# One kernel for a linear-attention recurrence, top-1 experts and a SwiGLU: first units and tail rearranged, the old state added by TensorE

## The chip, the core and the metric

The kernel runs on one core of one Trainium2 chip. What counts is the time of one execution on the device in microseconds (us). Five engines work side by side, each through its own instructions in program order: TensorE (PE in the profile, its weight loads PEld), VectorE (DVE), ScalarE (ACT), GpSimd (POOL) and SyncE (SP), whose queue issues most transfers. An instruction waits on semaphores for what it reads, and for the buffer that it writes.

## What is computed

Three layers in a row, for 2 batches of 768 tokens, in float32:

```
for t in range(S):                                   # attention, per batch and head (8 heads of 48)
    cur = einsum('bhd,bhe->bhde', u * k[t], v[t])
    y[t] = einsum('bhd,bhde->bhe', r[t], state + cur)
    state = w[t][..., None] * state + einsum('bhd,bhe->bhde', k[t], v[t])
x = y as 1536 rows of 384
expert = argmax(x @ w_gate)                          # top-1 of 8 experts, with a capacity, in token order
x = gate * (relu(x[expert] @ w1) @ w2)               # each expert 384 -> 1024 -> 384
out = (silu(x @ w_gate2) * (x @ w_val)) @ w_out      # 384 -> 1536 -> 384
```

## The kernel before

The recurrence is done in 12 units of 128 tokens, six to a batch (`UPB`). In a unit the products of the decays take two directions from the middle: `X` are running products and `R` running sums that stand for inverse products, started anew at every eighth token from `anch`, reciprocals of X. For unit u:

- `prep0` (ScalarE): copies of the decay `wm`, one place shifted, from the unit's load `dm`.
- `prep1` (VectorE): two scans X (L363), then two reciprocals `anch` (L368).
- `prep2` (VectorE): two scans R (L406), the products `M` of k and r with X and with R (L412, L415), and in `prep3` the product `rk` of r and k (L425).
- `scores`: eight matmuls `psA` of M with M (L460), two copies to `A` on ScalarE (L462), two masks on GpSimd (L463).
- `kgtok`: k of M transposed into `psT`, copied to `kgt` (L471, L473).
- `values`: y = A times v, plus M times the state `Sb` (L485, L490).
- `state`: eight matmuls P = kgt times v (L502); d, the decay of the whole unit (L505); `Sa` = P + old state (L510), except in a batch's first unit; `Sc` = Sa times d (L513). `expand` copies Sc into `Sb` on ScalarE (L521).
- `own` (GpSimd): `aV` = v times the diagonal term of the unit (L440). The diagonal comes from `rk` and u by matmuls in `gate_t`, a copy on ScalarE and `columns` (L570, L572).
- `xrow` (VectorE): x = y + aV (L527). `gate_t` transposes x for the gate.

The order is written out by hand (`manual_schedule`), one unit after the other. The loop's round u works on several units at once: `xrow(u - 1)`, `state(u)`, `scores(u + 1)`, `prep1(u + 2)`, `prep2(u + 2)`, `values(u)`, `own(u + 1)`. The input `dm` has three buffers, so `load_dm(u + 4)` in round u waits on SyncE's queue for rk of unit u + 1. `tick` puts one pending small step of the expert choice behind a VectorE instruction, and `flush` all of them. `warm(n)` is n bf16 matmuls whose result nobody reads.

The tail handles units 10 and 11 and the last groups of the choice: `four` (units 4 to 7), `two` (8, 9) and `last` (10, 11). For a group: logits, `choose` (largest, one-hot, exponentials and their sum), `count` (places within an expert by matmuls), `place`, then the rows weighted (`xg`) and scattered to the experts' places in HBM (`scatter`, GpSimd, L735). The first expert's rows of the last units don't take that way: `onehot` and `x0_add` (L810) sum them into PSUM by matmuls with a one-hot, where `x0_load` has brought what earlier units scattered. Of units 8 and 9 the weighted rows go in as float32, of 10 and 11 as two float32r halves (`x0_high` on ScalarE, `x0_low` on VectorE). `fill(us)` puts as many pieces of the weights' conversion into halves as `us` allows (ScalarE L207, VectorE L212). `early.close()` ends the buffers of the recurrence, behind which `load_raws` may load three more weight pieces.

## Time and profile before

| | us |
|---|---|
| median of 3 runs | 473.61 (472.63 to 474.22) |
| profiled execution | 477.16 |
| its span | 475.4 |
| PE busy | 454.4 (96%) |
| DVE busy | 335.0 (70%) |
| ACT busy | 239.8 (50%) |
| POOL busy | 72.6 (15%) |

The span runs from the first to the last instruction of the profiled execution. Busy shares are averages over stages that differ: the recurrence and the choice come first, then the experts (from 108.9 us), then the SwiGLU. In the chain of work that ended last, PE has 79% of the span and DVE 10%. PEclk is the granted clock of TensorE as a share of its upper level; "idle before" in brackets is how long the engine stood before an instruction, with what ended it.

### The profile page before, as it was taken

What the parts mean: (1) busy time and instruction counts of PE and PEld (TensorE: products, weight loads), DVE (VectorE), ACT (ScalarE), POOL (GpSimd) and SP (SyncE); (2) the same over time, 40 slices, a digit from 0 to 9 for tenths busy, and PEclk for the clock granted to TensorE, in tenths of its full rate; (3) what the DMA queues carried; (4) which work ended last, traced back from release to release, by engine and by line L of the source; (5) the groups of instructions that cost most, each with busy time, mean ns of one, the idle gap of its engine ahead of it and who ended that gap; (6) DMA issues with size and microseconds to landing.
All of it is one profiled execution on the core that took longest, in us unless ns stands there. A gap on an engine that the chain in (4) does not pass through costs nothing.

```text
span 475.4 us, 9312 instructions
## 1 busy us (share of the span) xinstructions
PE 454.4 (96%) x3572; PEld 401.8 (85%) x3572; DVE 335.0 (70%) x723; ACT 239.8 (50%) x560; POOL 72.6 (15%) x87
## 2 busy tenths in 40 slices
PE   7899889888999999999999999999999999999994
PEld 3587668678999999999988888888888888888884
DVE  8889999677798658559779966575868576434241
ACT  4466676636788677665455465353625333221220
POOL 3334445621000000000000370000000000003033
PEclk9899998959999999999999999999999999999999
DMA  7877996564989965027323425042200000001011
GB/s 241 234 236 205 361 270 186 184 215 135 293 272 345 305 239 175 24 67 219 115 77 123 71 64 122 11 123 77 66 2 1 1 0 0 1 0 68 0 68 66
DMA packets 33649, 62.57 MB, mean 132 GB/s; under 512 B 5216, under 2 KB 16992, under 8 KB 33600
## 3 DMA queue, kind: packets, MB, share of 16 engines
q1 hardware_dynamic: 31680, 57.20, 39.2%
q0 software_dynamic: 1920, 4.73, 2.7%
q8 instruction: 29, 0.48, 0.4%
q14 instruction: 20, 0.16, 0.1%
HBM read 52.48 MB, written 9.44 MB: 130 GB/s over the span
## 4 chain that ended last, share of the span: by engine, by line
PE 79%; DVE 10%; issue 4%; ACT 2%; DMA 2%; POOL 1%; another core or an unknown queue 0%; POOLq 0%; SPq 0%; DVEq 0%; ACTq 0%
PE psg L1381 31%; PE psu L1404 14%; PE psh L1270 14%; PE pso L1288 14%; DVE R L406 2%; DVE X L363 1%; PE psA L460 1%; DMA scr<-zrow 1%; POOL out L1416 1%; DVE M L415 1%; DVE M L412 1%; PE psx L1255 1%; PE y L490 1%; PE psW L449 1%; DVE rk L425 1%
## 5 line engine op out<-in xcount | busy, mean ns | idle before, releaser
L1381 PE MATMUL psg<-yb,wu 128*128 128x512 f32 x648 | 156.3, 395 | 0.0
L1381 PEld LDWEIGHTS psg<-yb,wu 128*128 128x128 f32 x648 | 121.5, 188 | 26.0
L1404 PE MATMUL psu<-wu,a 128*128 128x384 f32 x432 | 80.8, 336 | 0.0
L1404 PEld LDWEIGHTS psu<-wu,a 128*128 128x128 f32 x432 | 76.4, 188 | 2.9
L1270 PE MATMUL psh<-xe,wu 128*128 128x240 f32 x576 | 69.1, 277 | 1.4 <-DVE xe L816 1.4
L1270 PEld LDWEIGHTS psh<-xe,wu 128*128 128x128 f32 x576 | 66.2, 190 | 1.7 <-issue 1.6
L1288 PE MATMUL pso<-h,wu 128*128 128x240 f32 x576 | 66.4, 275 | 0.0
L1288 PEld LDWEIGHTS pso<-h,wu 128*128 128x128 f32 x576 | 65.3, 190 | 0.0
L1388 DVE TENSOR_TENSOR t<-t,psg 128x512 f32<-128x512 f32 x36 | 24.7, 686 | 52.6 <-PE psg L1381 35.6
L212 DVE TENSOR_TENSOR wu<-raw,wu 128x512 fp32r<-128x512 f32 x96 | 61.7, 683 | 0.0
L207 ACT CAST wu<-raw 128x512 fp32r<-128x512 f32 x96 | 55.0, 620 | 3.1 <-PE pso L1288 1.4
L1393 ACT CAST a<-t 128x512 fp32r<-128x512 f32 x36 | 22.3, 618 | 58.2 <-DVE t L1388 55.9
L1277 DVE SCALAR_TENSOR_TENSOR h<-psh,h 128x240 fp32r<-128x240 f32 x64 | 25.0, 403 | 24.1 <-ACT h L1276 23.8
L1303 POOL DMA_INDIRECT idl<-ids,dests x12 | 13.5, 1122 | 163.6 <-DVE bits L187 160.3
L1416 POOL DMA_INDIRECT out<-acc,idc x12 | 11.7, 973 | 174.1 <-DVE acc L1414 172.3
L207 ACT CAST wu<-bits 128x384 fp32r<-128x384 f32 x36 | 18.0, 514 | 40.0 <-DVE bits L200 39.2
L1387 ACT ACTIVATE t<-psg 128x512 f32<-128x512 f32 x36 | 21.4, 596 | 27.5 <-PE psg L1381 27.5
L1394 DVE TENSOR_TENSOR a<-t,a 128x512 fp32r<-128x512 f32 x36 | 24.8, 689 | 11.7 <-ACT a L1393 11.0
L1276 ACT ACTIVATE h<-psh 128x240 fp32r<-128x240 f32 x64 | 23.2, 372 | 11.0 <-PE psh L1270 10.2
L1414 DVE TENSOR_TENSOR acc<-psu,acc 128x384 f32<-128x384 f32 x24 | 12.9, 558 | 20.8 <-PE psu L1404 20.8
L462 ACT COPY A<-psA 128x512 f32<-128x512 f32 x24 | 12.9, 588 | 25.3 <-PE psA L460 23.0
L463 POOL TENSOR_SCALAR_AFFINE_SELECT A<-A 128x512 f32<-128x512 f32 x24 | 19.5, 834 | 27.5 <-ACT A L462 27.5
(153 smaller groups left out, 566.9 us busy)
## 6 DMA issues: line engine op xcount, KB each, us to landing
raw<-in_moe_w SPq DMA_DIRECT2D x32, 768.0 KB, 9.0
dm<-in_dm SPq DMA_DIRECT2D x18, 291.0 KB, 6.1
scr<-zrow SPq DMA_DIRECT2D x12, 384.0 KB, 5.4
raw<-in_moe_w_gate SPq DMA_DIRECT2D x6, 768.0 KB, 5.9
raw<-in_moe_w_val SPq DMA_DIRECT2D x6, 768.0 KB, 4.3
raw<-in_moe_w_out SPq DMA_DIRECT2D x6, 768.0 KB, 4.3
v<-in_tk SPq DMA_DIRECT2D x12, 192.0 KB, 6.7
dm<-in_dm SPq DMA_DIRECT2D x3, 512.0 KB, 5.7
```

Of the source, the lines that this page charges most:

```text
L207: nc.scalar.copy(out=slot_t[u % NSLOT][:, 0, c:c + n], in_=bits[i])
L212: nc.vector.tensor_tensor(out=w[:, 1, c:c + n], in0=bits.pop(i), in1=R(w[:, 0, c:c + n]), op=ALU.subtract)
L1270: nc.tensor.matmul(ps, w[:, a, k, c0:c0 + 128], xet[e][:, b, k, :], start=n == 0, stop=n == 8)
L1276: nc.scalar.activation(out=h[:, 0, :], in_=ps, func=AF.Relu)
L1277: nc.vector.scalar_tensor_tensor(out=h[:, 1, :], in0=ps, scalar=0.0, in1=R(h[:, 0, :]), op0=ALU.max, op1=ALU.subtract)
L1288: nc.tensor.matmul(ypt[e, d], w[:, a, f % 4, 128 * d:128 * d + 128], h[:, b, :], start=f == 0 and n == 0, stop=f == 7 and n == 2)
L1381: nc.tensor.matmul(gps[i][g], w[:, a, g, k, c0:c0 + 128], yb[t, k][:, c], start=a_ == k == 0, stop=a_ == k == 2)
L1387: nc.scalar.activation(out=t, in_=pg[0], func=AF.Silu)
L1388: nc.vector.tensor_tensor(out=t, in0=t, in1=pg[1], op=ALU.mult)
L1393: nc.scalar.copy(out=a[:, 0], in_=t)
L1394: nc.vector.tensor_tensor(out=a[:, 1], in0=t, in1=R(a[:, 0]), op=ALU.subtract)
L1404: nc.tensor.matmul(out_ps[t, j], att[i][:, c, 128 * j:128 * j + 128], w[:, a, f % 4, :], start=f % FP == 0 and n == 0, stop=f % FP == FP - ...
```

## The change

- `state`: the old state is added in PSUM by a matmul with the identity as the first into P; `Sa` is gone, and Sc reads P.
- `prep1` ends with X; the reciprocals are one instruction over both halves, in a function of its own, `anchored`.
- In a round, `prep0(u + 2)` and `prep1(u + 2)` come first, then `xrow(u - 1)`, `state(u)`, `anchored(u + 2)`.
- `own(u)` stands behind `scores(u + 1)`, in place of `own(u + 1)` at the round's end; `expand(u)` behind `gate_t`.
- Round 0: `values(0)` in one piece, then the diagonal of units 0 and 1 by two matmuls of 8 columns and one copy.
- Tail: `own(10)` on GpSimd behind the masks of unit 11; the first `fill` ahead of `own(11)`; `early.close()` and the loads behind it after `x0_load`; units 8 and 9 as float32r halves; the weighted rows, places and scatters of `two` later; the second `fill` behind `offsets`; two warming matmuls.

```
@@ prep1
-        A = halved(anch[u % 2], HC)
-        for h in range(2):
-            nc.vector.reciprocal(out=anchors(A, h, G - 1), in_=anchors(X, h, G + 1))
-            tick()
+    def anchored(u):
+
+        if u >= NU:
+            return
+        nc.vector.reciprocal(out=each8(anch[u % 2], HC), in_=each8(Xf[u], XW))
+        tick()
@@ state
+        if u % UPB:
+            nc.tensor.matmul(P, ident, Sc[u], start=True, stop=False, skip_group_check=True)
         for p in range(NP):
             for g in range(2):
                 c0 = D * (2 * p + g)
                 nc.tensor.matmul(P[64 * g:64 * g + 64, p, :], k[:, p, 64 * g:64 * g + 64], vts[u][:, c0:c0 + D],
-                                 start=True, stop=True, skip_group_check=True)
+                                 start=not u % UPB, stop=True, skip_group_check=True)
...
-        src = P
-        if u % UPB:
-            src = ap2.tile([128, NP, D], F32, tag="Sa", name="Sa")
-            nc.vector.tensor_tensor(out=src, in0=P, in1=Sc[u], op=ALU.add)
-            tick()
         s = Sc[u + 1] = ap2.tile([128, NP, D], F32, tag="Sc", name="Sc")
-        nc.vector.tensor_tensor(out=s, in0=src, in1=d.unsqueeze(2).to_broadcast([128, NP, D]), op=ALU.mult)
+        nc.vector.tensor_tensor(out=s, in0=P, in1=d.unsqueeze(2).to_broadcast([128, NP, D]), op=ALU.mult)
@@ the loop
         chosen, counted = ended.get(u - 2), ended.get(u - 3)
+        if u:
+            prep0(u + 2)
+            prep1(u + 2)
         xrow(u - 1)
         state(u)
-        if u:
-            prep0(u + 2)
+        anchored(u + 2)
         warm((7, 4)[u] if u < 2 else 3, ps1, "xT")
         scores(u + 1)
-        expand(u)
+        if u:
+            own(u)
         kgtok(u + 1)
-        if u:
-            prep1(u + 2)
...
+        expand(u)
         load_dm(u + 4)
...
             values(u)
             columns(u - 1, max(u - 2, 0), u + 1)
-            own(u + 1)
         else:
-            values(u, [0, 1])
+            values(u)
             for q in range(2):
-                columns(q, q, q)
-                own(q)
-            values(u, [2, 3])
+                to = logits_to(q)
+                nc.tensor.matmul(to[:, 0:E], gss.pop(q), fold[:, E:2 * E], start=True, stop=True)
+            a8 = gp.tile([128, 2, H], F32, tag="a82", name="a82")
+            nc.scalar.copy(out=a8, in_=lgt[group[0]][:, 0:2, 0:E])
+            for q in range(2):
+                a8s[q] = a8[:, q, :]
+            own(0)
@@ the tail
     scores(u + 1)
+    own(u)
...
-    early.close()
-    more_raws(RAWS[2])
-    load_raws(len(raws_))
     values(u, [2])
...
     xrow(u)
+    fill(1.2, 3.0)
     rows4[2]()
     own(u + 1, nc.vector)
...
     x0_load()
+    early.close()
+    more_raws(RAWS[2])
+    load_raws(len(raws_))
...
-    fill(1.2, 3.0)
     values(u + 1, [3])
-    for f in rows2:
-        f()
+    for i, q in enumerate(two):
+        x0_high(q, sm2[:, i, :])
     xrow(u + 1)
     logits(u)
+    warm(2)
...
-    x0_add(xgs[two[0]], R(hot[0][:, 0, :]), 0, first=True, ks=[0])
+    x0_add(xhl[two[0]][0], hot[0][:, 0, :], 0, first=True)
+    for i, q in enumerate(two):
+        x0_low(q, sm2[:, i, :])
+    for f in rows2:
+        f()
     judge()
...
     logits(u + 1)
-    for f in later:
-        f()
-    for q in two:
-        scatter(q)
-    flush()
-    fill(0.6, 3.0)
-    x0_add(xgs[two[0]], R(hot[0][:, 0, :]), 0, first=True, ks=[1, 2])
+    x0_add(xhl[two[1]][0], hot[0][:, 1, :], 0)
+    for i, q in enumerate(two):
+        x0_add(xhl[q][1], hot[0][:, i, :], 0)
...
     for f in (*bases, *sums):
         f()
+    flush()
+    for f in later:
+        f()
+    for q in two:
+        scatter(q)
...
-    x0_add(xgs[two[1]], R(hot[0][:, 1, :]), 0)
...
     offsets(one8)
+    fill(0.6, 3.0)
```

What that makes of the instructions' order. VectorE, from the cast of tri in round 0 to the R scans of unit 3 (the number behind wm and anch is the buffer's), before:

```order
L898 CAST tri<-before 128x128
L527 TENSOR_TENSOR x<-y,aV 128x384
L505 TENSOR_TENSOR d<-X 128x4
L510 TENSOR_TENSOR Sa<-psP,Sc 128x192
L513 TENSOR_TENSOR Sc<-Sa,d 128x192
L363 SCALAR_TENSOR_TENSOR X<-dm_110,xinit 128x264 x2
L368 RECIPROCAL anch_114<-X 128x32 x2
L406 SCALAR_TENSOR_TENSOR R<-wm_116,anch_114 128x256 x2
```

and with the change:

```order
L902 CAST tri<-before 128x128
L363 SCALAR_TENSOR_TENSOR X<-dm_110,xinit 128x264 x2
L527 TENSOR_TENSOR x<-y,aV 128x384
L510 TENSOR_TENSOR d<-X 128x4
L513 TENSOR_TENSOR Sc<-psP,d 128x192
L371 RECIPROCAL anch_114<-X 128x2x32
L409 SCALAR_TENSOR_TENSOR R<-wm_116,anch_114 128x256 x2
```

The two X scans moved ahead of x and the state, Sa is gone, and the reciprocal is one. The later units stand in the same order.

GpSimd, from the masks of unit 1 to those of unit 3 (A are the masked scores; the number behind a is the buffer of the diagonal), before:

```order
L463 AFFINE_SELECT A<-A 128x512 x2
L440 TENSOR_TENSOR aV<-v,a_355 128x384
L440 TENSOR_TENSOR aV<-v,a_360 128x384
L463 AFFINE_SELECT A<-A 128x512 x2
L440 TENSOR_TENSOR aV<-v,a_479 128x384
L463 AFFINE_SELECT A<-A 128x512 x2
```

and with the change:

```order
L466 AFFINE_SELECT A<-A 128x512 x2
L443 TENSOR_TENSOR aV<-v,a_361 128x384
L466 AFFINE_SELECT A<-A 128x512 x2
L443 TENSOR_TENSOR aV<-v,a_361 128x384
L466 AFFINE_SELECT A<-A 128x512 x2
L443 TENSOR_TENSOR aV<-v,a_472 128x384
```

The product aV is now that of the unit of the running round, one unit later than before, and is issued straight behind the masks of the next unit.

## Rows read from the trace of the kernel before

**Rows 1.** Busy us by engine (instructions), granted clock, DMA share, GB/s, in three stretches

```profile
50.00:60.00 10.00, 9.18 (x167) 7.10 (x165) 10.00 (x29) 7.58 (x21) 4.03 (x5) 1.00 1.03 355
60.00:70.00 10.00, 8.72 (x145) 6.38 (x141) 9.97 (x23) 7.76 (x25) 3.93 (x5) 1.00 1.07 273
96.00:104.00 8.00, 6.85 (x35) 5.68 (x36) 6.41 (x31) 3.32 (x9) 0.97 (x1) 0.50 0.63 216
```

**Rows 2.** VectorE's timeline, one unit: start us, us, engine, line, operation, tiles, shapes

```profile
36.29 0.55 DVE L527 TENSOR_TENSOR x<-y,aV 128x384 f32<-128x384 f32 x1
...
37.00 0.34 DVE L510 TENSOR_TENSOR Sa<-psP,Sc 128x192 f32<-128x192 f32 x1
37.38 0.36 DVE L513 TENSOR_TENSOR Sc<-Sa,d 128x192 f32<-128x192 f32 x1
37.66 1.30 DVE L363 TENSOR_TENSOR_SCAN X<-dm,xinit 128x264 f32<-128x264 f32 x2
38.87 0.54 DVE L368 RECIPROCAL anch<-X 128x32 f32<-128x32 f32 x2
39.33 1.70 DVE L406 TENSOR_TENSOR_SCAN R<-wm,anch 128x256 f32<-128x256 f32 x2
...
42.14 0.68 DVE L425 TENSOR_TENSOR rk<-dm 128x512 f32<-128x512 f32 x1
```

**Rows 3.** TensorE's timeline, the same unit

```profile
35.62 0.67 PE L502 MATMUL psP<-v,kgt 128*64 128x48 f32 x16
...
39.22 0.55 PE L541 MATMUL psx<-ident,x 128*128 128x128 f32 x3
...
41.75 0.67 PE L502 MATMUL psP<-v,kgt 128*64 128x48 f32 x16
```

**Rows 4.** Timeline of the first units, TensorE and VectorE; idle time before in brackets

```profile
18.35 0.40 PE L570 MATMUL lg<-fold,gs 128*128 128x16 f32 x2 [1.24 <-ACT gs L886]
...
21.49 0.56 DVE L527 TENSOR_TENSOR x<-y,aV 128x384 f32<-128x384 f32 x1 [1.72 <-POOL aV L440]
...
24.61 1.25 DVE L406 TENSOR_TENSOR_SCAN R<-wm,anch 128x256 f32<-128x256 f32 x2
...
29.35 0.56 DVE L527 TENSOR_TENSOR x<-y,aV 128x384 f32<-128x384 f32 x1 [1.27 <-PE y L490]
...
30.21 0.36 DVE L510 TENSOR_TENSOR Sa<-psP,Sc 128x192 f32<-128x192 f32 x1 [0.23 <-PE psP L502]
```

**Rows 5.** Timeline of GpSimd and VectorE, three places

```profile
47.71 0.98 POOL L440 TENSOR_TENSOR aV<-v,a 128x384 f32<-128x384 f32 x1 [0.83 <-ACT a L572]
...
47.92 1.31 DVE L415 TENSOR_TENSOR M<-dm,R 128x512 f32<-128x512 f32 x1
...
73.21 1.22 POOL L463 TENSOR_SCALAR_AFFINE_SELECT A<-A 128x512 f32<-128x512 f32 x2 [1.15 <-ACT A L462]
```

**Rows 6.** Timeline of the tail, TensorE, VectorE and ScalarE

```profile
89.18 0.84 PE L565 MATMUL lg<-wgs,xT 128*128 128x8 f32 x6
...
90.54 0.56 DVE L440 TENSOR_TENSOR aV<-v,a 128x384 f32<-128x384 f32 x1 [1.01 <-ACT a L572]
...
92.13 1.12 ACT L207 CAST wu<-raw 128x512 fp32r<-128x512 f32 x2
...
95.04 0.17 DVE L695 TENSOR_TENSOR t<-lg,ohs 128x16 f32<-128x16 f32 x1 [2.28 <-remote]
95.34 1.28 DVE L212 TENSOR_TENSOR wu<-raw,wu 128x512 fp32r<-128x512 f32 x2
...
97.15 0.90 PE L541 MATMUL psx<-ident,x 128*128 128x128 f32 x3 [3.50 <-DVE x L527]
...
97.63 0.17 DVE L680 COPY pcs<-lg 128x16 f32<-128x16 f32 x1
...
98.67 1.45 PE L565 MATMUL lg<-wgs,xT 128*128 128x8 f32 x6
...
108.89 1.27 PE L1270 MATMUL psh<-xe,wu 128*128 128x240 f32 x9 [1.40 <-DVE xe L816]
```

More of the change, by code (lines that the diff above doesn't have):

```diff
@@ L845, in build @@
     prep1(0)
+    anchored(0)
     make_identity(nc, ident)
@@ L859, in build @@
     prep1(1)
+    anchored(1)
     prep2(1)
@@ L967, in build @@
     values(u + 1, [1, 2])
-    c2, sums2, rows2, _ = chosen_of(two)
+    c2, sums2, rows2, sm2 = chosen_of(two)
     for f in c2:
```

## Prediction

> **What bounds the kernel now.** I read the engines' busy time by stretch first. While the recurrence runs over its twelve units, VectorE has no idle time left: 10.00 of 10 us from 50 to 60 and 9.97 from 60 to 70, while TensorE has 9.18 and 8.72 [rows 1]. The experts and the SwiGLU begin at 108.89 [rows 6] and are left alone by the diff. So what can move is the first 109 us: the units, and the tail from the last state to the first expert matmul.
>
> Next the order of time on VectorE in one unit [rows 2]: x of the unit before at 36.29, the state's three steps (d, Sa, Sc), the two X scans, two reciprocals (anch), two R scans, two products M, and rk at 42.14, behind which the next x comes at 42.8. That is 6.5 us with no gap. TensorE in the same unit goes from its state product at 35.62 to the next at 41.75: 6.13 us, also without a gap [rows 3]. The two are 0.4 us apart. A VectorE saving is worth what it takes only as long as TensorE, the masks on GpSimd and the loads don't come due first.
>
> Then the first units, which do wait [rows 4]: x of unit 0 waited 1.72 us for GpSimd's v*diagonal, because TensorE stood 1.24 us for ScalarE's copy of the diagonal rows (and then for the copied diagonal); x of unit 1 waited 1.27 us for y, and the sum behind it 0.23.
>
> **The change, part by part.**
>
> *First units.* Unit 0's values are now issued in one piece ahead of the diagonal, the diagonal of units 0 and 1 takes one copy, and VectorE runs X of unit 3 before it asks for x of unit 0. Where it stood from 19.77 to 21.49 VectorE would go on with X (37.66 to 38.87 in the later unit, 1.21), x 0.47, d about 0.15, Sc 0.36, anch 0.46 and reach R of unit 3 at 19.77 + 2.65 = 22.4, against 24.61 now [rows 2, 4]. If the load of that unit is not there yet the gain shrinks to nothing at the worst; I take 2.0. The wait of 1.27 + 0.23 in the next unit goes too, since TensorE, no longer held by the diagonal, is earlier there by more than that: 1.5. Together **3.5 us**.
>
> *The old state on TensorE.* Sa took VectorE 0.38 us from its start to that of Sc (37.00 to 37.38, [rows 2]). It goes from eight units; one lies inside the 2.0 above, so 7 x 0.38 = 2.7. Sc now reads the sum in PSUM itself; in unit 0 it already does and takes 0.36, as with Sa, so nothing is added. TensorE gets one more f32 matmul of 192 columns per unit. The trace has none; three of 128 columns against the same identity take 0.55, which makes 0.28 for 192, and the whole state product of eight takes 0.67 [rows 3]. Between these I take 0.3, near the lower end, the row with the same operand. TensorE's unit becomes 6.13 + 0.3 = 6.4 us. Four of the nine units are shorter for it (no state or no transposes at the batch's border), and without its own early waits [rows 4] it starts the run of units further ahead of VectorE than now, so I cost the 0.3 at nothing while VectorE is late; without that cover it would cost up to 7 x 0.3 = 2.1.
>
> *One reciprocal for two.* Two of 32 columns take 0.46 from the first's start to R's [rows 2]. One of 64 has the same elements and one start-up less. Between 0 and 0.23 per unit; I take 0.06, since the time seems to go with elements: 8 x 0.06 = **0.5**.
>
> *X ahead of row add and state.* It removes no work. What it buys is cover: 1.2 us of VectorE work stand between rk and the first thing that needs TensorE. In the steady units there is no wait to cover, so I count it at nothing there. Queued behind a late X are now x, the state and, on ScalarE, the masks' copies, since the copies of the decay for that unit are moved up with it.
>
> *v*diagonal behind the masks.* On GpSimd the product now follows the two masks directly instead of coming some 3 us after them. Nobody waits for it sooner: x of that unit is asked for a unit later. But it is where I expect to lose something. VectorE's M at 47.92 took 1.31 us, where rk, a product of the same size, takes 0.68 at 42.14, and it did so while v*diagonal ran on GpSimd (47.71 to 48.69) [rows 2, 5]: the 0.54 from GpSimd's end to M's end is about one product. M seems to have stood until GpSimd was done. The R pair at 39.33 lost 0.45 the same way to the masks (1.70 against 1.25 at 24.61, [rows 2, 4]). About 0.6 us per unit is lost so now. Put behind the masks, the product falls beside R and M, where it used to fall partly beside x and the state, which lost little. I take 0.3 more per unit, between 0 and the 0.98 of a whole product: 8 x 0.3 = **2.4 us lost**.
>
> [...]
>
> Units in all: 3.5 + 2.7 + 0.5 - 2.4 = **4.3 us** earlier at the last state.
>
> *Tail.* (a) Two weight halves of 1.28 us leave the path in front of x of unit 11 and move to the 1.01 us in which VectorE waits for the last diagonal [rows 6]: -1.2, and +0.2 where they don't fit. Their next two casts on ScalarE (1.12 us) then stand ahead of the exponentials of the same group, whose sum VectorE asks for next: +0.6. Net -0.4. [...] If it now keeps the clock (two warming matmuls are put there), -1.0. (c) The one-hot sums of units 8 and 9 become single-pass products that are done before the last group's one-hot exists, so the last ones start with it: -0.7, and the count is not behind them: -0.3. (d) Six small VectorE steps such as the copy of pcs (0.17, the next begun 0.1 behind it, [rows 6]) now stand between the last exponentials and the last places: +0.6 less the 0.2 that VectorE waited there. Sum between -0.2 (if the clock was never low in a run without the profiler) and -2.0; I take **-1.2**. The weight loads that were freed at 87 now queue on SyncE behind the read-back of the first expert's rows. The experts convert those loads some 20 us after they begin, so I cost this at nothing; if that cover went, they would be waited for.
>
> **What the sum is made against.** The profiled execution took 477.16 us, 475.4 of it the span, 3.55 above the median of 473.61. It holds a wait of 2.28 us at 95.04 for which the trace names no instruction [rows 6], and half clock behind it. I don't count on that wait in the median, nor on its going. So 4.3 + 1.2 = 5.5 is taken from the median: **468.1 us**.
>
> **Rivals.**
> 1. *No added collision, and the tail gives all.* 3.5 + 2.7 + 0.5 + 2.0 = 8.7: 464.9. For it: half of the collisions are a matter of phase, and the phase shifts anyway.
> 2. *The loads come due.* From 50 to 70 the DMA engines are at a share of 1.03 and 1.07, full [rows 1]; a unit's inputs are asked for when the unit three before is done with the buffer. If the transfers from 50 us on can only come 2 us earlier, X of unit 11 waits and with it ScalarE and the masks: units give 2.0, tail 1.2: 470.4. The 0.3 on TensorE coming due (2.1) gives 470.2, the same.
> 3. [...] With three GpSimd instructions in a row, each can stop VectorE for its whole length: two masks 1.22 (73.21) and a product 0.98 [rows 5] are 2.2 per unit against the 0.6 lost now, +1.6 x 9 = 14.4. Less 6.7 + 1.2 saved: 480.1. It decides from +0.9 per unit on. [...]
> 4. *No change.* The units end earlier and the tail gives it back, at the read-back and the row scatters in front of the experts: 473.6.
>
> **Chances.** Forecast 0.48, rival 1 0.20, rival 2 0.18, rival 3 0.08, rival 4 0.06. The range leaves out rival 3 and the far ends: 463.8 to 472.5. A difference under about 0.3% (1.4 us) can't be told from none here. Faster by more: 0.86 (forecast, rivals 1 and 2); within: 0.06; slower: 0.08.
>
> **What would show it.** In the trace of the changed kernel: R of unit 3 at about 22.5, no wait of x in units 0 and 1; Sc of the last state some 4.3 us earlier than now; x to x in a unit about 6.3; v*diagonal beside R or M with these at 1.3 rather than 0.7. A wait of X for its load would show rival 2, TensorE without a gap while VectorE waits for the state product its second half. The first expert matmul should stand near 103, or near 101 if the nameless wait is gone. [...]

## The result and the profile after

| us | before | changed |
|---|---|---|
| median | 473.75 (472.63 to 474.22) | 477.35 (477.04 to 477.99) |
| profiled execution, its span | 477.16, 475.4 | 477.18, 475.5 |
| last M of unit 11 begins | 83.13 | 78.49 |
| x of unit 11 | 96.54 | 88.74 |
| first expert matmul | 108.89 | 100.61 |
| first h of the experts | 110.25 | 108.42 |
| first expert matmul to the end of the span | 366.5 | 374.9 |

The changed kernel is **slower: ratio 1.0081, interval 1.0060 to 1.0102**. Forecast was 468.1. The two profiled spans are equal although the medians are not: the profiled execution of before took 3.4 us more than its median, and it holds the nameless wait of 2.28 us [rows 6] with a granted clock of 0.50 behind it [rows 1]. A trace of the old loop and tail without that wait (the run before_late, below, which defers the loads too) has the last M at 81.63, x of unit 11 at 92.86 and the first expert matmul at 105.06. Against it the changed kernel is 3.1, 4.1 and 4.45 us ahead. So in this pair of traces the part that the change works on became 4.45 us shorter, of 5.5 that were forecast, and **8.4 us were lost behind it**, in a stage that the prediction left alone.

That stage at its start. TensorE's timeline (start, us, tiles, count; in brackets the idle time ahead and what ended it):

```profile
100.61 4.30 PE L1284 MATMUL psh<-xe,wu 128*128 128x240 f32 x36 [1.15 <-ACTq L1223]
109.28 1.21 PE L1284 MATMUL psh<-xe,wu 128*128 128x240 f32 x4 [4.37 <-DVE h L1291]
```

The first four groups of nine matmuls run, fill the four buffers of `psh`, and TensorE stands, because nobody takes the results away. ScalarE's row, and the waits of 100 to 112 us (engine, line, what it waited for: total, times, longest):

```profile
108.42 0.37 ACT L1290 ACTIVATE h<-psh 128x240 fp32r<-128x240 f32 x1 [8.56 <-SPq L1223]
```

```profile
ACT h L1290 <- SPq L1223: 8.6, 1, 8.6
DVE h L1291 <- ACT h L1290: 8.5, 1, 8.5
```

The releaser is neither a matmul nor a load but SyncE's queue at L1223, the conditional block of the rare path that is not taken. What SyncE had in flight there, from its own timeline:

```profile
92.81 2.12 SPq L169 DMA_DIRECT2D raw<-in_moe_w  x4
108.73 0.82 SPq L1259 DMA_DIRECT2D xr<-scr  x2
```

What SyncE did at L1223 (duration in ns, smallest, median and largest; first and last start in us), and what it waited there in total, times, longest:

```profile
L1223 SPq EVENT_SEMAPHORE  x9: 17/17/17, 97.8 to 108.3; - x9
L1223 SPq COMPARE_BRANCH  x1: 70/70/70, 97.3 to 97.3; - x1
```

```profile
SPq L1223 <- SPq L1223: 10.6, 5, 3.0
```

The compare-and-branch itself took 0.07 us at 97.3. What held SyncE are the nine semaphore instructions that the program has behind it on the same line: they start between 97.8 and 108.3, and their waits end as the four deferred weight loads land, at 100.0, 103.0, 105.8 and 108.2 (the third by SyncE's semaphore, for its landing is not in the trace). SyncE issues its next transfer at 108.73. In the kernel before SyncE came to the same place at 105.6, 5.3 us after it had issued its last weight load, and waited there 0.5 us:

```profile
SPq L1209 <- SPq L1209: 0.5, 1, 0.5
```

By stretch (us, busy time and instructions of PE, PEld, DVE, ACT, POOL, then granted clock, DMA share, GB/s):

```profile
104.00:106.00 2.00, 0.91 (x9) 0.72 (x7) 0.00 (x0) 0.00 (x0) 0.00 (x0) 1.00 0.98 372
106.00:108.00 2.00, 0.00 (x0) 0.00 (x0) 0.00 (x0) 0.00 (x0) 0.00 (x0) 1.00 0.24 92
110.00:112.00 2.00, 1.35 (x5) 0.79 (x4) 2.00 (x6) 1.64 (x5) 0.00 (x0) 0.50 0.46 165
```

From 106 to 108 no compute engine works, and behind the pause TensorE's granted clock is 0.50. h is 6.45 us later than 1.36 us behind the first expert matmul, its distance in the kernel before (110.25 against 108.89); the other 2 of the 8.4 go with the half clock of 109 to 116 us, and were not measured apart.

The units, to set beside [rows 2] and [rows 3]. VectorE:

```profile
34.58 0.53 DVE L527 TENSOR_TENSOR x<-y,aV 128x384 f32<-128x384 f32 x1
...
35.28 0.36 DVE L513 TENSOR_TENSOR Sc<-psP,d 128x192 f32<-128x192 f32 x1
35.56 0.55 DVE L371 RECIPROCAL anch<-X 128x64 f32<-128x64 f32 x1
36.21 1.86 DVE L409 TENSOR_TENSOR_SCAN R<-wm,anch 128x256 f32<-128x256 f32 x2
...
39.18 0.68 DVE L428 TENSOR_TENSOR rk<-dm 128x512 f32<-128x512 f32 x1
...
40.99 0.53 DVE L527 TENSOR_TENSOR x<-y,aV 128x384 f32<-128x384 f32 x1
```

TensorE, and GpSimd:

```profile
31.27 0.57 PE L503 MATMUL psP<-Sc,ident 128*128 128x192 f32 x2
31.77 0.67 PE L507 MATMUL psP<-v,kgt 128*64 128x48 f32 x16
...
37.83 0.57 PE L503 MATMUL psP<-Sc,ident 128*128 128x192 f32 x2
```

```profile
35.03 1.24 POOL L466 TENSOR_SCALAR_AFFINE_SELECT A<-A 128x512 f32<-128x512 f32 x2 [4.51 <-ACT A L465]
36.24 1.28 POOL L443 TENSOR_TENSOR aV<-v,a 128x384 f32<-128x384 f32 x1
```

x to x is 6.41 (6.3 was named, 6.45 before). Sa is gone, but R takes 1.86, the single reciprocal is followed by R 0.65 later where two took 0.46, and the added matmul takes 0.50 from its start to the next, so that TensorE's unit is 6.56.

### The profile page after: what moved, and what is told of

It is laid out like the page before. It is cut to its first block, busy times and chain, and to the rows that moved or that the text cites. A ratio compares the mean times of both kernels' runs of the same rounds, so it can differ in the third digit from the quotient of the medians.

```text
span 475.5 us, 9303 instructions
## 1 busy us (share of the span) xinstructions
PE 452.9 (95%) x3579; PEld 400.9 (84%) x3590; DVE 332.6 (70%) x705; ACT 240.3 (51%) x561; POOL 69.3 (15%) x87
## 4 chain that ended last, share of the span: by engine, by line
PE 72%; issue 2%; DVE 1%; POOL 1%; POOLq 0%; ACT 0%; ACTq 0%
PE psg L1395 31%; PE psu L1418 14%; PE pso L1302 14%; PE psh L1284 13%; POOL out L1430 1%; PE psx L1269 1%; DVE acc L1428 0%; DVE wu L212 0%; POOLq L1534 0%; DVE h L1291 0%; ACT h L1290 0%; POOLq L1430 0%; ACTq L1290 0%
## 5 line engine op out<-in xcount | busy, mean ns | idle before, releaser
L1284 PE MATMUL psh<-xe,wu 128*128 128x240 f32 x576 | 72.4, 283 | 6.2 <-DVE h L1291 4.4
L1284 PEld LDWEIGHTS psh<-xe,wu 128*128 128x128 f32 x576 | 68.8, 196 | 7.1 <-DVE h L1291 4.6
L466 POOL TENSOR_SCALAR_AFFINE_SELECT A<-A 128x512 f32<-128x512 f32 x24 | 15.2, 657 | 44.3 <-ACT A L465 44.3
```

Source lines behind the costliest of these rows:

```text
L1284: nc.tensor.matmul(ps, w[:, a, k, c0:c0 + 128], xet[e][:, b, k, :], start=n == 0, stop=n == 8)
```

## The experiments

All runs but the last four are on chips where the kernel before has a median of 473.0 to 473.3; the last four are on another one, where it has 476.68. Ratios are to the kernel before on the same chip. Runs of one kernel differ by up to 6 us, and the mean granted clock goes with them (in split_two 0.990 to 0.994 in the five fastest runs, 0.978 and 0.980 in the two slowest), so places in the traces are given beside the medians. A place is read from one execution, and traces of one and the same loop differ too. The last M is at 81.42, 81.63 and 83.13 in the three with the old loop (before_fill, before_late, before). With the changed loop it is at 78.45 to 79.14 in the four in which the load of unit 11 was not late (split, changed, loads_behind, split_warm). Smaller differences between two single traces prove nothing by themselves.

**loads_behind: the four loads behind the branch.**

```
-    early.close()
-    more_raws(RAWS[2])
-    load_raws(len(raws_))
+    early.close()
+    more_raws(RAWS[2])
+    st["held"] = True
...
     xet[0] = xe0
+    del st["held"]
+    load_raws(len(raws_))
     x_load(1)
```

> The changed kernel, except that the weight loads which it defers until after the read-back of the first expert's rows are issued behind the branch of the rare path instead of ahead of it (no load is issued between the two places). Theory A: in the changed kernel ScalarE and VectorE wait with their first instruction behind the branch (107 us, 8.6 us of idle time) not for data that they read but because SyncE, on its way past the branch, waits for every load that it has in flight (landings at 100.0, 103.0, 105.8, 108.2) and only then lets the others on. Then this kernel has no such wait, the first h of the experts comes about 1.3 us after the first expert matmul near 100.6, and the time is 477.35 less 7 to 9: 468 to 470.5. Rival B: the experts' conversion needs those loads. They land later here, near 105 to 114, so the wait stays or grows: 477 or more.

Measured: 472.51 (10 runs), ratio 0.9984 (0.9965 to 1.0004). The wait is gone, though the loads land later, at 104.1 to 111.3:

```profile
101.66 11.30 PE L1286 MATMUL psh<-xe,wu 128*128 128x240 f32 x72 [1.54 <-ACTq L1225]
```

```profile
ACT h L1292 <- PE psh L1286: 6.4, 5, 3.5
```

SyncE's nine semaphore instructions now run from 97.8 to 98.4. So the conversions did not need those loads; SyncE's waits at the block did. Theory A holds and rival B is out. The gain is 4.8 (4.6 by the ratios), not 7 to 9: 72 matmuls take 11.30 us (8.70 in loads_early), with a granted clock of 0.50 until 107.7, and the first h waits for TensorE instead.

**loads_early: the loads in their old place, the rest as changed.**

```
     prep3(u + 1)
+    early.close()
+    more_raws(RAWS[2])
+    load_raws(len(raws_))
     values(u, [2])
```

> The changed kernel, except that the end of the recurrence's buffers and the weight loads behind it stand where they stood before the change, ahead of the third part of y of unit 10 (about 82 us). Theory A (SyncE waits at the branch for what is in flight): the loads land by about 92 to 96, before the branch, no wait at the first h: 468 to 470.5. But the scatters of units 4 to 7 and the read-back share the DMA engines with the loads again (in the kernel before they landed at 95 to 98 instead of 89 to 92), so the read-back may come last for the expert's rows: up to 3 us more, 471 to 473. Rival B (the conversion needs the loads): they come 10 us earlier than in the changed kernel, 468 to 470.5 too; this run does not tell A from B, the run with the loads behind the branch does.

Measured: 472.85 (10 runs), ratio 0.9989 (0.9965 to 1.0014). ScalarE does not wait at the block. The first expert matmul is at 102.83, 1.2 later than in loads_behind. Of that 0.9 stands already at the last M (79.37 against 78.50), where X of unit 11 had waited 1.10 for its load. The read-back is issued at 95.8 instead of 91.8, as the second half of the expectation had it, but TensorE waited only 0.4 for it.

**before_late: the kernel before with the deferral alone.** The edit is the reverse of the last one, made in the kernel before.

> The kernel before with one part of the change alone: the end of the recurrence's buffers and the weight loads behind it moved from ahead of the third part of y of unit 10 to behind the read-back of the first expert's rows. Theory A: the loads are issued near 95 to 99 and land one every 2.7 us until about 107 to 110, while the first expert matmul stands at about 105.5 to 108.9; ScalarE and VectorE wait at the branch until the last has landed, 2 to 6 us: 476 to 480. If the deferral is free, as the prediction had it: 473.75 within 1.4, or a little less as the scatters of units 4 to 7 have the DMA engines to themselves.

Measured: 480.48 (4 runs), ratio **1.0170** (1.0136 to 1.0203). TensorE and ScalarE:

```profile
105.06 4.30 PE L1270 MATMUL psh<-xe,wu 128*128 128x240 f32 x36 [1.16 <-ACTq L1209]
111.90 1.17 PE L1270 MATMUL psh<-xe,wu 128*128 128x240 f32 x4 [2.54 <-DVE h L1277]
```

```profile
111.04 0.37 ACT L1276 ACTIVATE h<-psh 128x240 fp32r<-128x240 f32 x1 [6.74 <-SPq L1209]
```

One part of the change, put into the old kernel, brings the same wait at the same place (its last load lands at 110.8) and costs 7.2 us. This settles where the loss is from.

**sum_on_vector: old state added by VectorE again** (on loads_behind).

```
-        if u % UPB:
-            nc.tensor.matmul(P, ident, Sc[u], start=True, stop=False, skip_group_check=True)
...
+            nc.vector.tensor_tensor(out=src, in0=P, in1=Sc[u], op=ALU.add)
```

> The kernel with the loads behind the branch, except that the old state is added by VectorE again (Sa, 0.34 us, next 0.38 later) and not by the matmul with the identity (0.50 from its start to the next). It stands against the kernel with the loads behind the branch. Theory A: in the changed kernel TensorE's unit is 6.55 us without a gap in units 2 to 4 and 8, where it was 6.13, so TensorE is the bound there and the sum on TensorE gains nothing: this kernel is within 1.0 of that one. Rival (VectorE is the bound, as the prediction had it): slower by 7 to 9 times 0.38, 2.7 to 3.4 us. A third: VectorE was relieved but TensorE's 0.5 costs more than it gives: faster by 1 to 2 us.

Measured: 473.62 (10 runs), x of unit 11 at 89.18 against 88.61. This kernel also has the flag changed in `values`, so y leaves out the state's part; the matmuls there are the same in number and shape. It pointed to no gain from the sum on TensorE; sum_again repeats it with `values` as it was.

**split: two loads early, two behind the branch.**

```
     prep3(u + 1)
+    early.close()
+    more_raws(RAWS[2])
+    load_raws(st["loaded"] + 2)
...
     xet[0] = xe0
+    load_raws(len(raws_))
```

> The changed kernel with the weight loads that it defers divided: two are issued where they all stood before the change (about 82 us), the other two behind the branch of the rare path. Theory A (SyncE waits at the branch for loads in flight): no wait there, as with all four behind it; the two early ones are done before the read-back of the first expert's rows needs the DMA engines, which in the run with all four early had put that read-back at 95.8 instead of 91.8, and the two late ones leave room for the rows of the second expert, which landed at 112.8 or later with four behind the branch. First expert matmul 100.5 to 102, time 470 to 472.5, against 472.5 and 472.9 for all behind and all early. If where the loads stand makes no difference once they are not in flight at the branch: 472.5 to 473.

Measured: 471.94 (12 runs, of which one at 476.98 is left out of the ratio), ratio 0.9977 (0.9954 to 1.0000), first expert matmul at 101.58. Not told apart from the two before it by time; it serves as the base of the next.

**split_two: two reciprocals again.** Only `anchored` differs.

> The kernel with the divided loads, but with the two reciprocals of 32 columns of the kernel before instead of one of 64. It stands against the kernel with the divided loads. The prediction had the single one 0.06 us per unit cheaper: then this one is 0.5 slower at the last M of unit 11. The trace of the changed kernel shows 0.65 us from the start of the single reciprocal to R (0.10 of it a gap: R reads what the instruction directly ahead of it writes), where two took 0.46 to R: then this kernel's units are up to 0.19 shorter, last M of unit 11 at 77 to 78 instead of 78.5, if VectorE sets the pace; and no earlier if TensorE does (6.55 us per unit without a gap).

Measured: 471.19 (12 runs), ratio 0.9958 (0.9930 to 0.9986). rk of unit 10 is at 71.87 against 72.35, but nearly all of that stands at rk of unit 4 already (32.17 against 32.58); from there on the six units take 39.70 and 39.77. With two reciprocals R starts 0.47 behind the start of the first instead of 0.65, and then takes 2.18 instead of 1.86:

```profile
35.44 2.18 DVE L413 TENSOR_TENSOR_SCAN R<-wm,anch 128x256 f32<-128x256 f32 x2
```

So the single reciprocal does not save the 0.5 that was counted; that it costs 0.4 in the first units is read from one pair of traces (raws_late and split_warm, a like pair, give 0.38 at the same place). The last M is at 79.73 against 78.45, because now a load has come due:

```profile
74.67 1.31 DVE L365 TENSOR_TENSOR_SCAN X<-dm,xinit 128x264 f32<-128x264 f32 x2 [2.06 <-DMA dm<-in_dm]
```

**split_own: v*diagonal at the end of the round again.**

```
-        if u:
-            own(u)
         kgtok(u + 1)
...
             columns(u - 1, max(u - 2, 0), u + 1)
+            own(u + 1)
```

> The kernel with the divided loads, but v*diagonal of the next unit stands at the end of the round on GpSimd, as in the kernel before, instead of the unit's own behind the masks. It stands against the kernel with the divided loads. [...] If the collision is only moved (R beside the masks and the product at 1.86 now, M beside the product at 1.31 before): within 0.5. If its new place is what the change gains by (x no longer waits for the product in units 0 and 1): up to 2 later.

Measured: 472.65 (12 runs), ratio 1.0003 (0.9978 to 1.0027); rk of unit 10 at 74.28 against 72.35, last M at 81.20 against 78.45. The unit is 6.73 instead of 6.42. VectorE and GpSimd in one unit:

```profile
36.13 0.42 DVE L512 TENSOR_TENSOR d<-X 128x4 f32<-128x4 f32 x1
...
39.35 1.32 DVE L420 TENSOR_TENSOR M<-dm,R 128x512 f32<-128x512 f32 x1
```

```profile
39.20 0.92 POOL L445 TENSOR_TENSOR aV<-v,a 128x384 f32<-128x384 f32 x1 [2.08 <-ACT a L574]
```

In the old place the product stops M (1.32 for 0.68) and the masks stop d (0.42 for 0.15): 0.91 per unit. Behind the masks it makes one stretch with them that R runs into: 1.86 for 1.28, 0.58. In this unit the move gains 0.3. From rk of unit 4 to rk of unit 10 it gains 0.6 in six units (39.77 against 40.41), and 1.3 in the units before (rk of unit 4 at 32.58 against 33.87). By time the two runs are not told apart (471.94 and 472.65).

**split_warm: fillers in two idle stretches of the tail.**

```
     count(last)
+    for _ in range(8):
+        nc.tensor.matmul(idle_ps, ones, idle_in, start=True, stop=True)
...
+    for _ in range(8):
+        nc.tensor.matmul(idle_ps, ones, idle_in, start=True, stop=True)
     for i, q in enumerate(last):
         x0_add(xhl[q][0], hot[0][:, 2 + i, :], 0)
```

> The kernel with the divided loads, and 8 bf16 matmuls of 192 columns, whose result nobody reads, at each of two places of the tail where TensorE stands idle: behind the counts of units 10 and 11 (0.85 us idle) and behind the totals (0.87 us). In the runs so far TensorE's granted clock falls to 0.50 at about 94 to 96 us and stays there for 3 to 13 us, into the first expert matmuls. Theory: the fall follows those idle stretches; if they are filled the clock stays at 1.00 and the last one-hot products and the first expert matmuls run at full rate: 1 to 3 us faster than the kernel with the divided loads. If the fall has another cause, or the fillers come too late: no faster than it, up to 0.5 slower.

Measured: **468.93** (6 runs), ratio 0.9923 (0.9901 to 0.9944): faster than both kernels. Stretches of the run split, and then of this one:

```profile
94.00:96.00 2.00, 1.38 (x6) 1.41 (x7) 1.96 (x8) 1.78 (x4) 0.12 (x1) 0.50 0.25 93
102.00:104.00 2.00, 2.00 (x11) 2.00 (x11) 0.00 (x0) 0.06 (x1) 0.00 (x0) 0.50 0.97 361
```

```profile
94.00:96.00 2.00, 1.65 (x21) 1.30 (x19) 1.87 (x12) 2.00 (x4) 0.00 (x0) 1.00 0.55 183
102.00:104.00 2.00, 2.00 (x20) 2.00 (x19) 2.00 (x5) 1.80 (x5) 0.00 (x0) 1.00 0.94 312
```

The granted clock is 1.00 in the whole tail of this trace, the first 72 expert matmuls take 8.78 us instead of 11.36, and from the first of them to the end it is 367.2 instead of 369.3.

**sum_again: old state added by VectorE** (on split_warm; the edit of sum_on_vector, in `state` alone).

> The kernel with the divided loads and the filler matmuls of the tail (468.9 us), except that the old state is added by VectorE (Sa) as in the kernel before. It stands against that kernel, whose last M of unit 11 began at 79.1 and first expert matmul at 100.0. If the sum on TensorE is worth 0.38 us per unit, as the prediction had it: last M of unit 11 2.5 to 3 later, time 471.5 to 472. If TensorE's 6.55 us per unit (0.50 of it the added matmul) sets the pace about as much as VectorE, as the first run of this edit pointed to: last M within 0.7, time 468.9 to 469.6.

Measured: 470.39 (9 runs), ratio 0.9934 (0.9909 to 0.9959). rk of unit 10 is at 72.41, earlier than with the sum on TensorE (73.19); 2.90 us are then lost to the load of unit 11, which landed at 75.9. The unit is 6.42 with Sa too. VectorE and GpSimd show why:

```profile
36.43 1.28 DVE L411 TENSOR_TENSOR_SCAN R<-wm,anch 128x256 f32<-128x256 f32 x2
```

```profile
34.43 1.22 POOL L468 TENSOR_SCALAR_AFFINE_SELECT A<-A 128x512 f32<-128x512 f32 x2 [4.30 <-ACT A L467]
35.62 0.93 POOL L445 TENSOR_TENSOR aV<-v,a 128x384 f32<-128x384 f32 x1
```

Without the added matmul the masks begin 0.22 behind x (34.21 to 34.43), with it 0.45 behind (changed) or 0.70 (split_warm). GpSimd is done at 36.55, when R has just begun, and R takes 1.28; with the matmul it takes 1.86 (changed) or 2.00 (split_warm). What Sa took (0.38), and what d and Sc lose beside the earlier masks, R gives back: from rk of unit 4 to rk of unit 10 it is 40.02 with Sa against 39.98 (split_warm) and 39.77 (split), where six units at 0.38 would be 2.3.

**x_behind: X behind x and the state again.**

```
-        if u:
-            prep0(u + 2)
-            prep1(u + 2)
         xrow(u - 1)
         state(u)
...
         kgtok(u + 1)
+            prep1(u + 2)
+            anchored(u + 2)
```

> The kernel with the divided loads and the filler matmuls of the tail (468.9 us), except that the copies of the decay, the X scans and the reciprocal stand behind x, the state and the scores' fillers again, where the kernel before had them. It stands against that kernel. The prediction counted X ahead of x at nothing in the steady units and at most at the two waits of the first ones (1.27 + 0.23 for x of unit 1, part of 1.72 for x of unit 0): then the last M of unit 11 is 0 to 2 later. If the move is what lets VectorE run without waits for TensorE's longer unit: over 2 later, with waits of x or Sc for TensorE in the steady units.

Measured: 470.47 (10 runs), ratio 0.9960 (0.9940 to 0.9980). rk of unit 4 is 0.4 later, rk of unit 10 1.4 (74.60), the last M 2.06 (81.20), the unit 6.74 instead of 6.55. No wait of x or Sc appears in the steady units. X now falls beside the masks: it takes 1.69 instead of 1.29, and R 1.66 instead of 2.00, so the collisions are about as long as before; what makes up the 0.2 per unit was not taken apart.

**raws_late: weight loads behind the last input load** (with two reciprocals).

```
         if u >= 4:
-            load_raws(2 * (u - 4) + 1)
+            load_raws(min(u - 3, 2) if u < 8 else 2 * (u - 4) + 1)
```

> The kernel with the divided loads and the filler matmuls of the tail (468.9 us), with two reciprocals of 32 columns instead of one of 64, and with four of the six weight loads of the recurrence issued behind the inputs of unit 11 (from 68 us on) instead of from 49 to 63. In the run with two reciprocals alone X of unit 11 waited 2.06 us for its load, which landed at 74.6: the loads had come due, and the reciprocals' gain of 0.5 us at rk of unit 10 was lost there. Theory: without the four weight loads ahead of it in the DMA engines the load of unit 11 lands before 72, the wait is gone, last M of unit 11 at 77.5 to 78.5 and 467.5 to 468.5. If the weight loads then come too late for the branch or the experts: a wait there, 469 or more. If the input loads are slow by themselves: the wait of X stays.

Measured: 468.49 (4 runs), ratio 0.9910 (0.9882 to 0.9938), last M at 78.99. The load of unit 11 has landed by 71.96, when ScalarE copies it without a wait, instead of 74.6, and X no longer waits for it (0.68 us for that of unit 3 remain). The wait went with the order of the loads. The last M is no earlier than with the single reciprocal (79.14 in split_warm), and the two runs are not told apart by time.

**quick: reciprocals and d ahead of x, one filler per unit.**

```
             prep1(u + 2)
+            anchored(u + 2)
+        decay(u)
         xrow(u - 1)
         state(u)
```

> As the run with the later weight loads, and in the loop the two reciprocals and d stand ahead of x, so that neither R nor Sc reads what the instruction directly ahead of it writes (gaps of 0.10 us each in the changed kernel), and one filler matmul per unit instead of three on TensorE (0.8 us to 0.2 to 0.4). If VectorE's gaps and TensorE's 6.55 us per unit are what holds the units: 0.2 to 0.3 us less per unit, last M of unit 11 at 75.5 to 77, time 465.5 to 467.5. If the loads of unit 11 or the masks set the pace: as the run with the later weight loads. If the clock falls for want of the fillers: half-rate stretches in the units and 469 or more.

Measured: 468.41 (4 runs), ratio 0.9904 (0.9881 to 0.9927). The last M is at 77.57, 1.4 earlier, but the granted clock falls from 1.00 to 0.50 at 87 us and the first expert matmul is at 101.25, 1.6 later. The units' gain was lost in the tail.

**loop_only: the changed loop with the old tail** (other chip).

> The changed kernel up to the end of the loop over the units, with the tail of the kernel before (weight loads in their old place, products of units 8 and 9 in float32, first conversion pieces in their old place); v*diagonal of unit 10 stands on GpSimd behind the masks, since the changed loop leaves it out. It stands against the kernel before (473.2) and against the changed kernel with all loads in their old place (472.9; last M of unit 11 at 79.4). By the prediction's terms the units are worth 4.3 and the tail 1.2: about 469. By the traces the units are worth 3.1 at the last M of unit 11 and the tail 1.3: 470 if the rest of the way to the experts is as before. If the loop's gain is given back in the old tail: 472 to 473.

Measured: 474.16 (10 runs) against 476.68, ratio 0.9946 (0.9928 to 0.9965), 2.5 us. The loop is worth something by itself. In its own trace the last M is at 80.30 (X of unit 11 waited 0.75 for its load), 1.1 ahead of before_fill on the same chip, and the nameless wait is there again. Between this run and loads_early only the tail differs, and the one with the old tail has the better ratio (0.9946 against 0.9989; the intervals touch, and the chips differ).

**round0: the first round as before** (split_warm, other chip).

> The kernel with the divided loads and the filler matmuls of the tail (468.9), with the first round's values and diagonal as in the kernel before: two parts of y, then a product, a copy and a diagonal for each of units 0 and 1, then the other parts of y. The prediction had 3.5 us for the first units, of X's and of this part together. If this part carries it: rk of unit 4 1.5 to 3.5 later than 33.2, time 470 to 472. If X ahead of x carries it: within 0.5 of 33.2, and 468.5 to 469.5.

Measured: 474.81 (10 runs), ratio 0.9974 (0.9945 to 1.0003) against 0.9923 of split_warm. rk of unit 4 is at 35.09 against 33.21, the last M at 81.70 against 79.14, and from 20 to 25 us the granted clock is 0.68, as in the kernel before from 20 to 30 (0.70). In this pair the first round's part is worth 1.9 to 2.6, the fall of the clock included.

**before_fill: fillers in the tail of the kernel before** (other chip).

```
     logits(u)
+    for _ in range(11):
+        nc.tensor.matmul(idle_ps, ones, idle_in, start=True, stop=True)
     for i in range(2):
```

> The kernel before with 11 filler matmuls of 192 columns behind the logits of unit 10, where TensorE stood 1.13 us for x of unit 11 (in the run with the late loads) ahead of the half-rate stretch of the tail. If that stretch (95 to 102 us, with the one-hot products of 240 columns in it) costs 2 to 3 us in the kernel before too and goes with the fillers: 470.5 to 472 instead of 473.2, and then some of what the best version gains over before is the fillers' alone. If it costs nothing there, because others set the end of the tail: 473.2 within 0.7.

Measured: 478.52 (10 runs), ratio 1.0039 (1.0022 to 1.0056): slower. The half-rate stretch stays (granted clock 0.50, about 97 to 104 us), and the nameless wait is there. So eleven fillers at this place gain nothing in the old tail; the two places of split_warm were not tried there.

This trace shows something else. Its first round is that of the kernel before, but here the clock did not fall in it. By stretch, the kernel before, then this run, and x of unit 1 in this run, which waits for nothing:

```profile
20.00:22.00 2.00, 2.00 (x34) 1.96 (x34) 0.51 (x2) 0.72 (x3) 1.42 (x2) 0.50 1.01 395
```

```profile
20.00:22.00 2.00, 2.00 (x37) 1.29 (x36) 1.21 (x5) 0.73 (x3) 1.29 (x2) 1.00 0.96 328
```

```profile
27.38 0.55 DVE L527 TENSOR_TENSOR x<-y,aV 128x384 f32<-128x384 f32 x1
```

rk of unit 4 is at 33.16 here, against 34.22 in before_late and 35.69 in the kernel before, where the clock fell at about 20 us.

**quick_fill: quick with more fillers** (other chip): two per unit, and six of 192 columns behind the counts of units 8 and 9.

> The run with the reciprocals and d ahead of x, with two filler matmuls per unit instead of one and six more of 192 columns behind the counts of units 8 and 9. In the run without them the granted clock fell to 0.50 at 87 us, behind 0.67 us of idle TensorE, and the units' gain (last M of unit 11 at 77.6 instead of 79.0) was lost by the first expert matmul (101.3 instead of 99.6). If the fall follows that idle stretch: no half rate in the tail, first expert matmul at 98 to 98.7, time 466.5 to 467.3, faster than all so far. If it does not: half rate again, 467.8 to 469.

Measured: 471.15 (4 runs) against 476.68, ratio **0.9882** (0.9845 to 0.9918). The half rate (granted clock 0.50) came all the same, from 93 to 99 us, behind 1.5 us of idle TensorE that end at 91.3. By ratio it is the best of all, but raws_late, quick and this one are not told apart by their intervals.

## Why the prediction was wrong, point by point

- **The deferred loads** are the step that failed: "The experts convert those loads some 20 us after they begin, so I cost this at nothing; if that cover went, they would be waited for." The cover was true and beside the point: in loads_behind the conversions went on while those loads landed at 104.1 to 111.3. What waited was SyncE at the conditional block, and with it ScalarE and VectorE: h came 6.45 us late, and 8.4 were lost from the first expert matmul on. No rival held it; rival 3, with its 480.1, had the right sign by another cause. The edit's queue was followed to its data, not to the next point at which all engines meet. With this step taken back (loads_behind, loads_early, split) it is 471.9 to 472.9, so it explains 4.5 to 5.4 of the 9.2 us by which the time missed 468.1. The other 4 are the terms below and the clock in the tail: only with 16 filler matmuls that are not in the change (split_warm) do the same loop and tail give 468.9. That this is 0.8 from the forecast is luck.
- **First units**, 3.5: at rk of unit 4 it was 34.22 (before_late) to 32.76, 1.5 us. Neither x of unit 0 nor x of unit 1 waits any more, as named, but R of unit 3 is at 23.68, not 22.5: rk of unit 2 took 1.31 beside v*diagonal of unit 0 (GpSimd, 18.78 to 19.77), and X stood behind it. The term added up waits that stand in a stretch of half clock (granted 0.50 from 20 to 26 us in the kernel before) and took them for the order's. Where the old first round kept the clock (before_fill), the wait of 1.27 + 0.23 for unit 1 is not there, and rk of unit 4 is 0.4 behind the changed kernel; at rk of unit 5 it is 1.5 (40.66 against 39.18), as in before_late. Three of the four traces with the old first round lost the clock there and none of the 14 with the new one, so part of the gain may be the clock's; how much is open.
- **Old state on TensorE**, 2.7: nothing. From rk of unit 4 to rk of unit 10 it is 40.02 with Sa on VectorE, and 39.77 (split) or 39.98 (split_warm) without. What failed is "I cost the 0.3 at nothing while VectorE is late": the matmul takes 0.50, and by it the masks reach VectorE's R (1.86 instead of 1.28).
- **One reciprocal**, 0.5 gained: nothing gained, and 0.4 lost by unit 4. R reads what the instruction just ahead writes, and starts 0.10 behind its end; with two, R starts 0.18 earlier, but in the steady units it then takes 2.18 instead of 1.86. "The time seems to go with elements" looked at the instruction and not at its reader.
- **X ahead**, nothing: 1.4 at rk of unit 10 and 2.06 at the last M, in one pair of traces. It was priced as cover for waits alone.
- **v*diagonal behind the masks**, 2.4 lost: 1.9 gained at rk of unit 10 (1.3 of it by unit 4), 2.75 at the last M. In these traces the sign was wrong; by time nothing is told apart. "Put behind the masks, the product falls beside R and M, where it used to fall partly beside x and the state": it falls beside R alone, and leaves M free. M takes 1.32 beside the product (split_own) and 0.68 without it (the changed kernel), and the sum drawn from such rows counted what the new neighbours lose and too little of what the old ones get back.
- **The units' sum**, 4.3: 3.1 at the last M against before_late, and between 2.3 and 4.7 over all pairs of the traces named at the head of the experiments. None of its terms came out as sized and one had the wrong sign, and they cancelled. The parts do not add either: each sets the phase between VectorE and GpSimd that the others are priced in (the masks begin 0.22 to 0.70 behind x).
- **The tail**, 1.2: from the last M to the first expert matmul 23.4 (before_late) and 22.1, 1.3. But with other places for the loads the same new tail takes 23.2 (loads_behind), 23.1 (split) and 23.5 (loads_early), and by time loop_only, with the old tail, is no slower than loads_early, so a gain of the tail is not shown. Its lower bound of 0.2 is not the sum of its terms either: without the 1.0 for a kept clock they give 1.0. No run shows that 1.0: the granted clock falls from 1.00 to 0.50 at about 95 all the same, two warming matmuls are not enough, and what the runs show in its place is that a clock of 1.00 in the whole tail goes with 367.2 us from the first expert matmul to the end (split_warm), where split, with 0.50 from 94 to 107, has 369.3. The one-hot sums of units 8 and 9 did become single-pass: at L810 the kernel before has 12 matmuls for their 6 float32 sums, the changed one 24 for the 24 float32r halves of units 8 to 11.
- **The loads of unit 11** (rival 2) were not due in the changed kernel, by 0.1 us: ScalarE's copies waited for them until 73.09, and X begins at 73.13 without a wait. In loads_early, split_two and sum_again they were (1.10, 2.06 and 2.90 us), and raws_late shows how the wait goes. The program of loads_early is the same up to there, so this differs from one execution to the next.
- **The nameless wait** was rightly kept out of the sum, but it belongs to the old tail more than was thought (below).

## What to carry to other kernels

Look at what the program puts at a conditional block, even one that is never entered: here the nine semaphore instructions at it ended only at 108.3 us, with the last of SyncE's four loads in flight (landed at 108.2), and took 0.6 us where those loads were issued behind it (loads_behind). So ask for every transfer that is moved whether it has landed when its queue comes to the next such block, and issue those that have not behind it. Before a wait is priced, read the granted clock of its stretch (from 20 to 22 us 0.50 in one trace of the old first round and 1.00 in another). Where an instruction takes longer beside one of another engine, as M here with 1.32 us instead of 0.68, price a move by both neighbours, old and new, and by the phase that the move itself sets; what a change saves in one instruction may be what the next then loses, as here Sa's 0.38 us and R's 1.86 instead of 1.28. And a sum that comes out right with wrong terms proves none of them; only undoing the parts one at a time does.

## What the runs showed of the hardware that was not expected

- **The conditional block that is not entered waited for its queue's loads, and not by its branch instruction.** In the changed kernel and in before_late SyncE's compare-and-branch took 0.07 us (at 97.3 and 101.0). The nine semaphore instructions behind it ended only when its last load had landed (108.2, 110.8), and ScalarE's next instruction, and with it VectorE's, waited for SyncE; TensorE went on until the four buffers of `psh` were full (36 matmuls in 4.30 us). In split and loads_behind, with the loads landed or issued behind the block, the nine took 0.6 us, and in loads_early they waited for one load until 102.1, before ScalarE had anything to do behind the block. The compare-and-branch takes 68 to 84 ns on four engines and 392 to 397 ns on TensorE's queue (the kernel before and the changed one); by that alone the deferral would have cost nothing, and before_late shows 7.2 us. Why the program has the nine semaphore instructions there was not tried.
- **TensorE's granted clock in the tail** fell from 1.00 to 0.50 in most traces, at some point between 87 and 98 us and for 3 to 13 us, behind stretches in which TensorE had stood, such as 0.85 and 0.87 us in split or 0.67 in quick. The four traces without it (split_warm, sum_again, x_behind, raws_late) all have the fillers in the last two idle stretches; quick, round0 and quick_fill have the same fillers and lost the clock. So the fillers help and do not settle it; what decides is open. With and without the fall the same stretch from the first expert matmul to the end took 369.3 (split) and 367.2 (split_warm).
- **The nameless wait returns.** VectorE's waits from 84 to 100 us in loop_only, and in before_fill:

```profile
DVE t L695 <- remote: 2.9, 1, 2.9
```

```profile
DVE t L695 <- remote: 2.4, 1, 2.4
```

  With that of the kernel before, these are the three traces with the old tail and the loads ahead of it. Neither the old tail with late loads (before_late) nor the new tail with early loads (loads_early) has it. What delays it is open, and so is how many unprofiled runs of the kernel before hold it.
